# Attention on one core: weighted sums in six bursts a unit, by a written-out order, and one ring of seven PSUM banks

## The chip, the cores and the metric

The kernel runs on one core of one Trainium2 chip. The metric is the device time of an execution in microseconds (us). The engines are named as in the profile: PE (TensorE matmuls), PEld (TensorE weight loads), DVE (VectorE), ACT (ScalarE), POOL (GpSimd), SP (SyncE, which issues most DMAs).

## The reference

A parallel block over one sequence of 2048 rows of width 448: the input, plus multi-query attention (16 heads of width 28 that share one key and one value head), plus an MLP that normalises its input once more.

```python
S, D, H, Dh, F = 2048, 448, 16, 28, 1792
xn = layernorm(x)
q = (xn @ wq)  # 16 heads of 28
k, v = xn @ wk, xn @ wv  # one head each
p = softmax(q k^T * Dh ** -0.5)
A = (p v, heads side by side) @ wo
B = gelu(layernorm(xn) @ w1 + b1) @ w2 + b2
return x + A + B
```

## The kernel before, in words

The program has three stages. The first normalises the input and projects it to q, k and v. The second is the MLP, whose result, with the input and the second bias added, goes to a DRAM buffer `ad` (line 604). The third, attention, is the one that the change rewrites, and it lasts from about 352 us to the end.

**Units.** Attention is cut into 16 units. A unit is 512 query rows (a chunk `c`, four of them) and a group `g` of four heads. Of a unit there are 16 key tiles `kt` of 128 keys, and for each key tile four score products, one a head `j`: 64 a unit.

**Scores and exps.** `scores` (line 616) takes a PSUM bank, multiplies a key tile with one head's queries into it (line 618, one 128x512 matmul; the trace names the two kinds of bank `s` and `t`), and ScalarE writes the exponentials to an SBUF tile `p` (line 620). The queries carry an extra row that subtracts an estimate of the row maxima. Banks come from `score_bank` (line 613): by turns from `ring_a` (three banks, `s`) and from `ring_b` (three banks, `t`), so a score waits for the exp of the score six before it. The first eight scores (`EARLY`) run while the MLP's last matmuls run.

**Weighted sums.** `pv(u, kt)` (line 729) multiplies the four `p` tiles of a key tile with the values and a column of ones, each into its own 32 partitions of one bank `po` (line 733). The program has four such matmuls a key tile; the trace shows each of them twice, so that a burst of two key tiles stands there as x16. After 16 key tiles `po` holds the unit's unnormalised result and its denominators.

**Normalising.** `norm_jobs` (line 707) has three pieces. The first: DVE copies `po` to `oc` (line 710), and a DMA takes the denominators out of it (`rc`, line 712). The second: DVE saves them in `sums`, takes reciprocals (lines 714 and 715), and DMAs spread these through DRAM (`ld`, line 716) to all partitions (`tr`, four DMAs, line 719). The third: DVE multiplies (line 721) and rounds (`oth`, line 723), POOL makes the rest `otl` (line 724).

**Output projection.** `o_parts` (line 691) takes a unit's four row tiles in turn: three 128x448 matmuls into one bank (lines 696, 698, 700), then DVE adds the bank to a row tile that was loaded from `ad` (line 702). For the last head group the row tile goes out (line 704). The bank is the pool `mo`, which has one bank. It also serves `block_max` (line 537), which `find_max` runs once a unit for the next unit: a matmul (line 539), then on DVE a transpose, a maximum, a negation and a transpose back (lines 540 to 546), and a DMA of the row into the next unit's queries (line 547).

**The order.** Attention runs in steps of eight scores, eight steps a unit. At the end of each step stands a burst of two key tiles' weighted sums, those of the step before. Other jobs are put at a step and at a slot among its eight scores (`at`, line 768): the load of the next unit's queries at a unit's first step (`load_unit`, line 549: `qm` by four DMAs, then `xh` by four), the maxima at its fourth, and the matmuls of the output projection one at a time by the table `PARTS`, from the fifth step of the unit after on. All DMAs but two at the very end are issued by SP, in program order.

**The end.** `last_norm` (line 736) normalises the last unit without DMAs and adds its rows. `flag` checks that no denominator lies outside limits; if one does, a branch that is not taken here computes attention again.

PSUM has eight banks. In attention they are six for scores, one `mo`, one `po`. During the MLP they are three of `ring_a`, `mo`, and four that the MLP accumulates in.

Of the kernel before, what the change touches and what calls it, by code (L numbers as in the profile page):

```python
# [10 lines left out]
F32 = mybir.dt.float32  # L11
F32R = mybir.dt.float32r
I32 = mybir.dt.int32
# [3 lines left out]
PSUM = bass.MemoryType.PSUM  # L17

P = 128
S, D, H, DH, F = 2048, 448, 16, 28, 1792  # L20
NT = S // P
CT = 4
NCH = NT // CT
CW = CT * P
# [7 lines left out]
HD = D // 2  # L32
WEIGHTS = 28
EARLY = 8
PARTS = 2, 1, 2, 1, 2, 2, 2
LIMITS = 0.25, 2.0 ** 40


# [1 line left out]
def block_kernel(ctx, tc, x, wq, wk, wv, wo, w1, b1, w2, b2, out):  # L40
# [4 lines left out]
    def f(t):  # L45
        return t.bitcast(F32)

    keep = ctx.enter_context(tc.tile_pool(name="keep", bufs=1))
    mo = ctx.enter_context(tc.tile_pool(name="mo", bufs=1, space=PSUM))
    dram = ctx.enter_context(tc.tile_pool(name="dram", bufs=1, space=bass.MemoryType.DRAM))  # L50
    xt_p = ctx.enter_context(tc.tile_pool(name="xt", bufs=len(KEPT)))
    xl_p = ctx.enter_context(tc.tile_pool(name="xl", bufs=len(KEPT)))
# [56 lines left out]

    def mtile(shape):  # L110
        return mp.tile(shape, F32, name="m")

    def bank(shape):
        return mo.tile(shape, F32, name="mo")

    def rawtile(shape):
        return tmp.tile(shape, F32, name="raw", bufs=2)
# [116 lines left out]
    def second_of_first():  # L234
        ts = slice(0, CT)
        r = rstd(lnrq[:, 1:2, ts], lnp[:, ts, 1], CT, (True,))
        next(r)
        yield
        next(r)
        shift(True, ts)  # L240
        yield
# [199 lines left out]
    g = stats(1)  # L441
# [16 lines left out]
    g = second_of_first()  # L458
# [13 lines left out]
    for c in range(NCH):  # L472
        if c + 1 < NCH:
            center, turn = norm_parts(c + 1, False, bank=lambda shape: (qbank, mtile)[next(turns) % 2](shape))
        for i in range(4):
# [16 lines left out]
            if (c, i) == (NCH - 1, 3):  # L492
                _, end = evac()
# [6 lines left out]
            if i in ((1, 3), (1, 2), (1, 3), (0, 2))[c]:  # L500
                n = 2 * c + (i - 1 if c == 1 else i // 2 if c == 3 else i // 3)
# [12 lines left out]
    units = [(c, g) for c in range(NCH) for g in range(NG)]  # L514
    NU = len(units)
# [18 lines left out]
    def blocks(t):  # L534
        return t.rearrange("p (a b) -> p a b", b=32)

    def block_max(keys, dst):
        pm = bank([P, CW])
        pe.matmul(pm, keys, qm, start=True, stop=True)  # L539
        dve.transpose(tm, pm)  # L540
        dve.tensor_reduce(dst, blocks(tm), axis=AX.X, op=ALU.max)
# [7 lines left out]
    def load_unit(u):  # L549
        qss[u] = qst[u % 2]  # L550
        load_strips(u)
        load_q(u, qss[u])

    def find_max(u):
        mr = keep.tile([P, CW // 32], F32, name="mr", bufs=2)
        block_max(kd, mr)
        shift_rows(u, mr)

    ring_a = ctx.enter_context(tc.tile_pool(name="ra", bufs=3, space=PSUM))

    def spare():
        return ring_a.tile([P, CW], F32, name="s")
# [46 lines left out]
    turn_s = itertools.count()  # L609
    ring_b, ps = [], {}  # L610
    todo = [(u, kt, j) for u in range(NU) for kt in range(NT) for j in range(4)]

    def score_bank():
        return ring_b[0].tile([P, CW], F32, name="t") if ring_b and next(turn_s) % 2 else spare()

    def scores(u, kt, j):
        s = score_bank()
        pe.matmul(s, ks[:, kt * P:(kt + 1) * P], qss[u][:, j, :], start=True, stop=True)  # L618
        p = early.pop(0) if early else att.tile([P, CW], F32, name="p", bufs=WEIGHTS)
        act.activation(p, s, AF.Exp, scale=SCALE)  # L620
        ps[u, kt, j] = p
# [3 lines left out]
    for c in range(len(KEPT), NCH):  # L625
        g = norm_gen(MLP_ORDER[c], lambda shape: ring_a.tile(shape, F32, name="s"))
        for i in range(2 * CT + 1):
            norms[NF * (c - 1) + 4 + i] = lambda g=g: next(g, None)
    for n in range(len(mslots) + 2):
        c, ft = mslots[n] if n < len(mslots) else (NCH, n - len(mslots))  # L630
# [24 lines left out]
        if n >= len(mslots):  # L655
            t = f(xl_p.tile([P, 4, CW], F32R, name="xl"))
# [33 lines left out]

    def o_parts(c, g):
        oth, otl = ots[c, g]
        for k in range(CT):
            po = bank([P, D])
            ts = slice(k * P, (k + 1) * P)
            pe.matmul(po, oth[:, ts], woh[:, g, :], start=True, stop=False)  # L696
            yield
            pe.matmul(po, oth[:, ts], wol[:, g, :], start=False, stop=False)  # L698
            yield
            pe.matmul(po, otl[:, ts], woh[:, g, :], start=False, stop=True)  # L700
            a = rows[c, k]
            dve.tensor_add(a, a, po)  # L702
            if g == NG - 1:
                nc.sync.dma_start(ov[:, CT * c + k, :], a)
            yield

    def norm_jobs(u, po):
        c, g = units[u]
        oc = att.tile([P, CW], F32, name="oc")
        dve.tensor_copy(oc, po)  # L710
        rc = att.tile([P, CW // 32], F32, name="rc")
        nc.sync.dma_start(rc, oc[0:P:32, :])
        yield
        dve.tensor_copy(sums[:, u, :], rc)
        dve.reciprocal(rc, rc)
        nc.sync.dma_start(ld.rearrange("h (i e) -> (h i) e", e=CW // 32), rc)
        tr = att.tile([P, CW], F32, name="tr")
        for h in range(4):
            nc.sync.dma_start(tr[32 * h:32 * h + 32, :], ld[h:h + 1, :].to_broadcast([32, CW]))
        yield  # L720
        dve.tensor_mul(oc, oc, tr)
        oth, otl = ots[c, g] = [att.tile([P, CW], F32R, name=n, bufs=3) for n in ("oth", "otl")]
        dve.tensor_copy(oth, oc)
        pool.tensor_sub(otl, oc, f(oth))  # L724
        yield

    pos = {}

    def pv(u, kt):
        if kt == 0:  # L730
            pos[u] = op.tile([P, CW], F32, name="po")
        for j in range(4):
            pe.matmul(pos[u][32 * j:32 * j + 32, :], vs[:, kt, :], ps[u, kt, j],  # L733
                      start=(kt == 0), stop=(kt == NT - 1))
# [28 lines left out]
                dve.tensor_add(a, a, outs[k][:, 0:D])  # L763
            (nc.scalar if k % 2 else nc.sync).dma_start(ov[:, CT * c + k, :], a)

    side = {}

    def at(step, job, slot=4):
        side.setdefault((min(step, PER * NU - 1), slot), []).append(job)

    PER = NT // 2
    for u in range(NU):
        c, g = units[u]
        if u + 1 < NU:
            at(PER * u, lambda u=u: load_unit(u + 1))
            at(PER * u + 3, lambda u=u: find_max(u + 1))
        if g == 0:
            at(PER * (u + 1), lambda c=c: load_rows_of(c))
    at(3, split_out)
    waiting = []  # L780

    def weighted():
        for u, kt in waiting:
            pv(u, kt)
        if not waiting or waiting[-1][1] < NT - 1 or u == NU - 1:
            return
        norm = norm_jobs(u, pos.pop(u))
        next(norm)
        for d in (1, 3):
            at(PER * (u + 1) + d, lambda: next(norm), 3)  # L790
        parts = []

        def part():
            if not parts:
                parts.append(o_parts(*units[u]))
            next(parts[0])

        for d, n in enumerate(PARTS if u < NU - 2 else (3, 3, 3, 3)):
            for slot in (1, 5, 7)[:n]:
                at(PER * (u + 1) + 4 + d, part, slot)  # L800

    bad = keep.tile([P, 2], F32, name="bad")
    worst = keep.tile([P, 2], F32, name="worst")
# [3 lines left out]
    def extremes(src, to):  # L807
        dve.tensor_reduce(to[:, 0:1], src, axis=AX.X, op=ALU.max)
        dve.tensor_reduce(to[:, 1:2], src, axis=AX.X, op=ALU.min)

    def flag(last):
        extremes(last.bitcast(I32), bad)
        dve.tensor_tensor(bad[:, 0:1], bad[:, 0:1], worst[:, 0:1], op=ALU.max)
        dve.tensor_tensor(bad[:, 1:2], bad[:, 1:2], worst[:, 1:2], op=ALU.min)
        dve.tensor_scalar(bad[:, 0:1], bad[:, 0:1], hi, 0.0, op0=ALU.is_gt, op1=ALU.add)
        dve.scalar_tensor_tensor(bad[:, 0:1], bad[:, 1:2], lo, bad[:, 0:1], op0=ALU.is_lt, op1=ALU.add)
        pf = bank([1, 1])
        pe.matmul(pf, bad[:, 0:1], one[:, 0:1], start=True, stop=True)
        return lambda: dve.tensor_copy(count, pf)

    done = EARLY
    for step in range(PER * NU):
        for i in range(8):
            if done:
                done -= 1
            else:
                scores(*todo.pop(0))
            for job in side.pop((step, i), []):
                job()
        weighted()  # L830
        waiting = [divmod(n, NT) for n in (2 * step, 2 * step + 1)]
    extremes(sums[:, 0:NU - 1, :].rearrange("p u e -> p (u e)").bitcast(I32), worst)
    weighted()
    last_norm(NU - 1, pos.pop(NU - 1), flag)

    outside = nc.values_load(count)
# [47 lines left out]
```

## Time and profile before

| | |
|---|---|
| three runs | 906.68, 907.39 and 907.75 us |
| median | 907.39 us |
| the profiled execution's own time | 906.84 us |
| its span, from first to last instruction | 905.0 us |
| TensorE clock that the throttle granted, mean | 0.996 of full speed |
| PE busy, share of the span | 98% |
| ACT busy | 75% (32.19 us of a steady unit's 33.97) |
| DVE, POOL busy | 32%, 17% |

The span is what the profile covers; the execution's own time is 1.8 us longer. Matmuls are pipelined, and their lengths overlap: what a matmul costs on PE is read from the distance of the starts. A row of the timeline names the engine, the line of the kernel, and output<-inputs. A weight load (PEld) has a row of its own beside the matmul that it serves; it stands with the same line.

### The profile page before, as it was taken

Reading aid. Unit: us, or ns where it says so; the run is one execution under the profiler, and the core shown is the slowest. Engines: PE = TensorE matmul, PEld = TensorE weight load, DVE = VectorE, ACT = ScalarE, POOL = GpSimd, SP = SyncE. Lnnn points to the kernel's source line nnn. Section 1 sums busy time; section 2 is a strip of 40 time slices with the busy share of each in tenths; the row PEclk is TensorE's granted clock in tenths of the full one; section 3 lists DMA queues with packets and bytes.
Section 4 is the critical chain, followed back from the end, with each engine's and each line's share of the span. In section 5 each row is a group of like instructions: output and inputs, shape, how many; then the busy total and the mean of one; then the engine's idle time right before and its main releaser. Section 6 shows DMA issues by size and latency. Waiting matters only on the chain.

```text
span 905.0 us, 13020 instructions
## 1 busy us (share of the span) xinstructions
PE 891.2 (98%) x4925; PEld 567.7 (63%) x4925; DVE 294.0 (32%) x554; ACT 676.5 (75%) x1285; POOL 156.1 (17%) x149
## 2 busy tenths in 40 slices
PE   9989999999999999999999999999999999999996
PEld 8867888888888887454554554554554554554552
DVE  7865454334344442222122122122122122122113
ACT  5764443333443337999999999999999999999993
POOL 6443243243235331000000000000000000000000
PEclk9999999999999999999999999999999999999998
DMA  9791112002002204312202222202221202222001
GB/s 279 219 282 51 42 62 82 1 1 81 21 21 57 66 12 114 106 24 54 52 24 54 86 72 54 52 24 54 89 68 54 53 24 54 81 76 54 1 13 43
DMA packets 42041, 60.03 MB, mean 66 GB/s; under 512 B 10794, under 2 KB 26744, under 8 KB 41976
## 3 DMA queue, kind: packets, MB, share of 16 engines
q1 hardware_dynamic: 40568, 58.60, 22.9%
q8 instruction: 40, 0.66, 0.3%
q10 hardware_dynamic: 1408, 0.57, 0.2%
q14 instruction: 25, 0.20, 0.1%
HBM read 43.16 MB, written 14.80 MB: 64 GB/s over the span
## 4 chain that ended last, share of the span: by engine, by line
PE 94%; DVE 2%; ACT 2%; issue 1%; DMA 0%; POOL 0%; ACTq 0%; DVEq 0%; POOLq 0%
PE po L733 26%; PE s L618 16%; PE m L598 14%; PE t L618 13%; PE s L180 11%; PE qp L180 3%; PE mo L696 1%; PE mo L698 1%; PE mo L700 1%; PE s L185 1%; PE s L183 1%; PE qp L304 1%; DVE hz L581 0%; PE mo L539 0%; DVE hx L583 0%
## 5 line engine op out<-in xcount | busy, mean ns | idle before, releaser
L620 ACT ACTIVATE p<-s 128x512 f32<-128x512 f32 x508 | 315.5, 621 | 26.7 <-PE s L618 22.4
L620 ACT ACTIVATE p<-t 128x512 f32<-128x512 f32 x508 | 319.5, 629 | 0.0
L733 PE MATMUL po<-p,vs 128*32 128x512 f32 x2032 | 244.1, 598 | 0.0
L618 PE MATMUL s<-xh,ks 128*128 128x512 f32 x516 | 216.6, 420 | 0.0
L618 PE MATMUL t<-xh,ks 128*128 128x512 f32 x508 | 200.4, 395 | 0.2 <-DVE a L603 0.2
L618 PEld LDWEIGHTS s<-xh,ks 128*128 128x128 f32 x516 | 97.0, 188 | 121.6 <-ACT p L620 105.6
L733 PEld LDWEIGHTS po<-p,vs 128*32 128x32 f32 x2032 | 53.1, 109 | 121.5 <-issue 116.1
L579 ACT ACTIVATE hx<-s,b1t 128x512 f32<-128x512 f32 x56 | 38.5, 688 | 113.8 <-PE s L185 104.2
L702 DVE TENSOR_TENSOR row<-row,mo 128x448 f32<-128x448 f32 x60 | 37.3, 621 | 235.7 <-PE mo L700 234.5
L587 POOL TENSOR_TENSOR hl<-hx,hh 128x512 fp32r<-128x512 f32 x56 | 77.5, 1384 | 183.2 <-DVE hh L586 174.2
L724 POOL TENSOR_TENSOR otl<-oc,oth 128x512 fp32r<-128x512 f32 x15 | 19.3, 1289 | 500.6 <-PE t L618 236.5
L618 PEld LDWEIGHTS t<-xh,ks 128*128 128x128 f32 x508 | 95.5, 188 | 14.0 <-ACT p L620 1.9
L598 PE MATMUL m<-w2l,hh 128*128 128x448 f32 x224 | 82.6, 369 | 0.9 <-DVE w2l L382 0.9
L598 PE MATMUL m<-w2h,hh 128*128 128x448 f32 x224 | 82.4, 368 | 0.5 <-DVE a L603 0.4
L598 PE MATMUL m<-w2h,hl 128*128 128x448 f32 x224 | 82.0, 366 | 0.7 <-POOL hl L587 0.7
L581 DVE SCALAR_TENSOR_TENSOR hz<-hz,hx 128x512 f32<-128x512 f32 x56 | 45.4, 811 | 104.6 <-ACT hz L580 104.4
L582 ACT ACTIVATE hz<-hz 128x512 f32<-128x512 f32 x56 | 35.4, 632 | 49.8 <-DVE hz L581 49.8
L180 PE MATMUL s<-xh,w1h 128*128 128x512 f32 x168 | 65.7, 391 | 2.4 <-DVE qe L405 2.4
L180 PE MATMUL s<-xl,w1h 128*128 128x512 f32 x168 | 65.8, 392 | 0.0
L180 PE MATMUL s<-xh,w1l 128*128 128x512 f32 x168 | 65.8, 391 | 0.0
L583 DVE SCALAR_TENSOR_TENSOR hx<-hz,hx 128x512 f32<-128x512 f32 x56 | 39.1, 698 | 43.3 <-ACT hz L582 43.3
L710 DVE COPY oc<-po 128x512 f32<-128x512 f32 x15 | 10.4, 692 | 115.4 <-PE po L733 115.4
(162 smaller groups left out, 896.8 us busy)
## 6 DMA issues: line engine op xcount, KB each, us to landing
xh<-qd SPq DMA_DIRECT2D x64, 224.0 KB
qd<-qe SPq DMA_DIRECT2D x24, 256.0 KB
a<-in_A_x_dram SPq DMA_DIRECT2D x24, 224.0 KB
tr<-ld SPq DMA_DIRECT2D x60, 64.0 KB
ad<-a SPq DMA_DIRECT2D x16, 224.0 KB
qm<-qd SPq DMA_DIRECT2D x64, 56.0 KB
row<-ad SPq DMA_DIRECT2D x16, 224.0 KB
raw<-in_B_w_dram SPq DMA_DIRECT2D x7, 448.0 KB
```

The lines of the kernel that those rows point to most:

```text
L180: pe.matmul(ps, w, v, start=(n == 0), stop=False)
L579: act.activation(hx, ph, AF.Identity, bias=b1t[:, ft:ft + 1])
L581: dve.scalar_tensor_tensor(hz, hz, 1.0, hx, op0=ALU.add, op1=ALU.mult)
L582: act.activation(hz, hz, AF.Tanh, scale=GELU[1])
L583: dve.scalar_tensor_tensor(hx, hz, 1.0, hx, op0=ALU.add, op1=ALU.mult)
L587: pool.tensor_sub(hl, hx, f(hh))
L598: pe.matmul(m2[k], h[:, k * P:(k + 1) * P], w[:, ft, :], start=(ft == 0 and i == 0), stop=(ft == NF - 1 and i == 2))
L618: pe.matmul(s, ks[:, kt * P:(kt + 1) * P], qss[u][:, j, :], start=True, stop=True)
L620: act.activation(p, s, AF.Exp, scale=SCALE)
L702: dve.tensor_add(a, a, po)
L724: pool.tensor_sub(otl, oc, f(oth))
L733: pe.matmul(pos[u][32 * j:32 * j + 32, :], vs[:, kt, :], ps[u, kt, j], start=(kt == 0), stop=(kt == NT - 1))
```

## The change

The table `PARTS` and the steps go. The order of a unit is written out in `ORDER`, a string of tokens: `s7` is seven scores, `P2` is the weighted sums of two key tiles, `o` is a whole row tile of the output projection (all three matmuls and the add), `m` is the maxima of the next unit. A unit has 64 scores, 16 key tiles, 4 row tiles and one `m` as before, and its weighted sums come as P2, P3, P2, P3, P3, P3. Scores run eight ahead, as before.

The pieces of `norm_jobs` are placed by key tiles now: the first behind a unit's 16th, the second two key tiles later, the third six later, and the row tiles join the queue of `o` tokens eight later. So a unit's row tiles are spread over the next two units: two on the last two `o` of the next one, two on the first two `o` of the one after. Unit 0 has none, unit 1 only the last two. In the last unit an `o` takes up to four row tiles.

The pool `mo` goes. `ring_a` has four banks instead of three, and scores, maxima, row tiles and the final check all take banks from one ring of seven (four `s`, then three `t`), so each waits for the user of the bank seven before it. In the MLP stage `ring_a` alone is there, with four banks.

`load_unit` and `load_rows_of` stand ahead of a unit's order. `split_out`, two DVE operations that split the projection's weights, moves in unit 0 from behind the first maxima to behind the token `s9`, ahead of them.

```diff
-PARTS = 2, 1, 2, 1, 2, 2, 2
+ORDER = "s7 P2 s9 P3 s4 o s o s9 P2 m s9 P3 s9 P3 s3 o s9 P3 s4 o"
...
-    mo = ctx.enter_context(tc.tile_pool(name="mo", bufs=1, space=PSUM))
...
     def block_max(keys, dst):
-        pm = bank([P, CW])
+        pm = score_bank()
...
-    ring_a = ctx.enter_context(tc.tile_pool(name="ra", bufs=3, space=PSUM))
+    ring_a = ctx.enter_context(tc.tile_pool(name="ra", bufs=4, space=PSUM))
...
     def score_bank():
-        return ring_b[0].tile([P, CW], F32, name="t") if ring_b and next(turn_s) % 2 else spare()
+        return ring_b[0].tile([P, CW], F32, name="t") if ring_b and next(turn_s) % 7 > 3 else spare()
...
-            po = bank([P, D])
+            po = score_bank()[:, 0:D]
             ts = slice(k * P, (k + 1) * P)
             pe.matmul(po, oth[:, ts], woh[:, g, :], start=True, stop=False)
-            yield
             pe.matmul(po, oth[:, ts], wol[:, g, :], start=False, stop=False)
-            yield
             pe.matmul(po, otl[:, ts], woh[:, g, :], start=False, stop=True)
...
     def weighted():
-        for u, kt in waiting:
-            pv(u, kt)
...
+        n = next(place)
+        u, kt = divmod(n, NT)
+        pv(u, kt)
+        if kt == NT - 1 and u < NU - 1:
+            norm = norm_jobs(u, pos.pop(u))
+            next(norm)
+            soon(n + 2, lambda: next(norm))
+            soon(n + 6, lambda: next(norm))
+            soon(n + 8, lambda: parts.append(o_parts(*units[u])))
+        for job in at.pop(n, ()):
+            job()
...
+    def soon(n, job):
+        at.setdefault(n, []).append(job)
...
+    def part():
+        if parts and next(parts[0], True):
+            parts.pop(0)
+            part()
...
+    def token(kind, u):
+        if kind == "s" and todo:
+            scores(*todo.pop(0))
+        elif kind == "P":
+            weighted()
+        elif kind == "m" and u + 1 < NU:
+            find_max(u + 1)
+        elif kind == "m":
+            extremes(sums[:, 0:u, :].rearrange("p u e -> p (u e)").bitcast(I32), worst)
+        elif kind == "o":
+            for _ in range(CT if u == NU - 1 else 1):
+                part()
...
-        pf = bank([1, 1])
+        pf = score_bank()[0:1, 0:1]
...
+    for u in range(NU):
+        if u + 1 < NU:
+            load_unit(u + 1)
+        if units[u][1] == 0:
+            load_rows_of(units[u][0])
+        for n, word in enumerate(ORDER.split()):
+            for _ in range(int(word[1:] or 1)):
+                token(word[0], u)
+            if (u, n) == (0, 2):
+                split_out()
```

First place, PE in a steady unit. Before, a step of eight scores with two single projection matmuls, from one burst to the next:

```order
L733 MATMUL po<-p,vs 32x512 x8
L618 MATMUL s<-xh,ks 128x512
L618 MATMUL t<-xh,ks 128x512
L696 MATMUL mo<-xl,oth 128x448
L618 MATMUL s<-xh,ks 128x512
...
L698 MATMUL mo<-xl,oth 128x448
...
L733 MATMUL po<-p,vs 32x512 x8
```

Now, in the same engine's list, the stretch `P3 s4 o s o s9 P2 m` of a steady unit:

```order
L727 MATMUL po<-p,vs 32x512 x12
L614 MATMUL s<-xh,ks 128x512 x4
L692 MATMUL t<-xl,oth 128x448
L693 MATMUL t<-xl,oth 128x448
L694 MATMUL t<-xl,otl 128x448
L614 MATMUL t<-xh,ks 128x512
...
L614 MATMUL s<-xh,ks 128x512 x4
L614 MATMUL t<-xh,ks 128x512 x3
L614 MATMUL s<-xh,ks 128x512 x2
L727 MATMUL po<-p,vs 32x512 x8
L535 MATMUL s<-qm,kd 128x512
```

Bursts of 8 matmuls behind every eighth score became bursts of 8 or 12 with 9, 11 or 14 scores between them; the three matmuls of a row tile stand together, in a bank of the scores' ring, and so does the matmul of the maxima (L535).

Second place, DVE in a steady unit. Before, between the copy of `po` and the maxima (`oc`, `sums`, `rc` and `oth` belong to the normalising, `row` to the adds of the projection, `tm` and `mr` to the maxima):

```order
L710 COPY oc<-po 128x512
L702 TENSOR_TENSOR row<-row,mo 128x448
L714 COPY sums<-rc 128x16
L715 RECIPROCAL rc<-rc 128x16
L702 TENSOR_TENSOR row<-row,mo 128x448
L721 TENSOR_TENSOR oc<-oc,tr 128x512
L723 CAST oth<-oc 128x512
L540 STREAM_TRANSPOSE tm<-mo 128x512
```

Now:

```order
L704 COPY oc<-po 128x512
L696 TENSOR_TENSOR row<-row,t 128x448
L708 COPY sums<-rc 128x16
L709 RECIPROCAL rc<-rc 128x16
L696 TENSOR_TENSOR row<-row,t 128x448 x2
L715 TENSOR_TENSOR oc<-oc,tr 128x512
L717 CAST oth<-oc 128x512
L536 STREAM_TRANSPOSE tm<-s 128x512
```

One more add stands ahead of the multiplication that waits for `tr`, and the transpose behind it reads a bank of the ring instead of `mo`.

Third place, SP's queue of DMAs over a steady unit. Before:

```order
L547 DMA xh<-tm 1x4x512
L532 DMA qm<-qd_73 28x512 x4
L526 DMA xh<-qd_73 28x4x512 x2
L526 DMA xh<-qd_74 28x4x512 x2
L712 DMA rc<-oc 128x1x16
L716 DMA ld<-rc 128x16
L719 DMA tr<-ld 32x512 x4
```

Now:

```order
L543 DMA xh<-tm 1x4x512
L706 DMA rc<-oc 128x1x16
L528 DMA qm<-qd_70 28x512 x4
L522 DMA xh<-qd_70 28x4x512 x2
L522 DMA xh<-qd_71 28x4x512 x2
L710 DMA ld<-rc 128x16
L713 DMA tr<-ld 32x512 x4
```

The eight loads of the next unit's queries moved from ahead of `rc` to between `rc` and `ld`.

More of the change, by code (lines that the diff above doesn't have):

```diff
@@ L111, in mtile @@
         return mp.tile(shape, F32, name="m")
-    def bank(shape):
-        return mo.tile(shape, F32, name="mo")
     def rawtile(shape):
@@ L764, in last_norm @@
             (nc.scalar if k % 2 else nc.sync).dma_start(ov[:, CT * c + k, :], a)
[L766 to L780, printed above, removed]
-    def weighted():
-        for u, kt in waiting:
-            pv(u, kt)
[L785 to L800, printed above, removed]
+    at, parts, place = {}, [], itertools.count()
+    def soon(n, job):
+        at.setdefault(n, []).append(job)
+    def weighted():
+        n = next(place)
[25 more added lines that the diff above has]
+                part()
     bad = keep.tile([P, 2], F32, name="bad")
@@ L816, in flag @@
         dve.scalar_tensor_tensor(bad[:, 0:1], bad[:, 1:2], lo, bad[:, 0:1], op0=ALU.is_lt, op1=ALU.add)
-        pf = bank([1, 1])
+        pf = score_bank()[0:1, 0:1]
         pe.matmul(pf, bad[:, 0:1], one[:, 0:1], start=True, stop=True)
         return lambda: dve.tensor_copy(count, pf)
[L821 to L833, printed above, removed]
+    for u in range(NU):
[8 more added lines that the diff above has]
+                split_out()
     last_norm(NU - 1, pos.pop(NU - 1), flag)
```

## The prediction

> **What bounds the kernel now.** I read the chain of work that ended last on the page first, then a table by stretches, then the timeline of the attention stage.
>
> ```profile
> PE 94%; DVE 2%; ACT 2%; issue 1%; DMA 0%; POOL 0%; ACTq 0%; DVEq 0%; POOLq 0%
> ```
>
> The chain is TensorE nearly throughout, so what shortens its queue shortens the run, unless a wait takes its place. The stretches below (us, then busy us and count for PE, PEld, DVE, ACT, POOL, then clock and DMA) are unit 0, whose weighted sums run beside no output projection, and a steady unit.
>
> ```profile
> 354.24:386.08 31.84, 31.84 (x194) 14.92 (x193) 5.98 (x7) 31.56 (x65) 0.00 (x0) 1.00 0.50 126
> 419.73:453.70 33.97, 33.97 (x206) 17.10 (x205) 7.02 (x13) 32.19 (x66) 1.29 (x1) 1.00 0.17 43
> ```
>
> ScalarE is a close second: busy 32.19 of 33.97 us in a steady unit, 31.56 of 31.84 in unit 0. Next, one step of a steady unit in the timeline (start, length, engine, line, output<-input): 8 scores, 2 single matmuls of the output projection (mo), 1 burst of weighted sums (po), and the exps on ACT.
>
> ```profile
> 504.57 1.92 PE L733 MATMUL po<-p,vs 128*32 128x512 f32 x16
> ...
> 506.43 0.50 PE L618 MATMUL s<-xh,ks 128*128 128x512 f32 x1
> 506.76 0.40 PE L618 MATMUL t<-xh,ks 128*128 128x512 f32 x1
> 506.96 0.60 ACT L620 ACTIVATE p<-s 128x512 f32<-128x512 f32 x1
> 506.99 0.37 PE L696 MATMUL mo<-xl,oth 128*128 128x448 f32 x1
> 507.20 0.39 PE L618 MATMUL s<-xh,ks 128*128 128x512 f32 x1
> 507.20 0.19 PEld L618 LDWEIGHTS t<-xh,ks 128*128 128x128 f32 x1
> 507.43 0.39 PE L618 MATMUL t<-xh,ks 128*128 128x512 f32 x1
> 507.45 0.59 ACT L620 ACTIVATE p<-t 128x512 f32<-128x512 f32 x1
> ...
> 508.56 0.39 PE L618 MATMUL t<-xh,ks 128*128 128x512 f32 x1
> 508.88 1.92 PE L733 MATMUL po<-p,vs 128*32 128x512 f32 x16
> 510.32 0.67 ACT L620 ACTIVATE p<-t 128x512 f32<-128x512 f32 x1
> 511.27 0.60 ACT L620 ACTIVATE p<-s 128x512 f32<-128x512 f32 x1 [0.29 <-PE s L618]
> ```
>
> Starts count here, since lengths overlap. Scores start 0.23 apart (507.20, 507.43), a projection matmul takes 0.21 (506.99 to 507.20), exps start 0.48 apart (507.45 to 510.32 is six steps). The last burst of all has four key tiles instead of two:
>
> ```profile
> 887.90 3.64 PE L733 MATMUL po<-p,vs 128*32 128x512 f32 x32
> ```
>
> 3.64 less 1.92, by two, is 0.86 us a key tile, and it shows that a longer burst keeps that pace.
>
> **Part 1, fewer bursts.** The step from 504.57 to 508.88 lasts 4.31. Less 8 x 0.23, 2 x 0.21 and 2 x 0.86 leaves 0.33, which belongs to the burst itself: 0.09 ahead of it (508.56 to 508.88 is 0.32, not 0.23), 0.14 inside (504.57 to 506.43 is 1.86, not 1.72), 0.10 behind its first score (506.43 to 506.76 is 0.33, not 0.23). Before, 128 steps give 127 bursts (the first step has none). The changed order has 6 a unit, 96 in all. 31 x 0.33 = 10.2 us less; the counts of scores, key tiles, projection matmuls and maxima stay.
>
> **Part 2, waits for banks that go.** With the one mo bank, a row tile's first matmul waits for the add that empties it, once a unit, where DVE copies po first:
>
> ```profile
> 520.14 0.62 DVE L702 TENSOR_TENSOR row<-row,mo 128x448 f32<-128x448 f32 x1
> 520.86 0.42 PE L696 MATMUL mo<-xl,oth 128*128 128x448 f32 x1
> 521.12 0.39 PE L618 MATMUL s<-xh,ks 128*128 128x512 f32 x1
> ```
>
> The mo matmul holds PE 0.26, not 0.21: 0.05 x 14 units = 0.7 less. Steps without projection also wait, for one of six score banks:
>
> ```profile
> 369.19 0.59 ACT L620 ACTIVATE p<-t 128x512 f32<-128x512 f32 x1
> ...
> 369.83 0.19 PEld L618 LDWEIGHTS t<-xh,ks 128*128 128x128 f32 x1 [0.22 <-ACT p L620]
> 369.88 0.44 PE L618 MATMUL t<-xh,ks 128*128 128x512 f32 x1
> 370.25 1.07 PE L733 MATMUL po<-p,vs 128*32 128x512 f32 x8
> ```
>
> 369.88 to 370.25 is 0.37, not 0.32: 0.05 x some 9 steps = 0.5 less. The row also prices such a wait: the weight load starts 0.05 after the exp's end (369.78), and a load with nothing ahead costs 0.10 (as behind a burst), so a score runs 0.15 after its bank's exp has ended. At the stage's start the second score waits for MLP banks:
>
> ```profile
> 351.52 0.63 PE L618 MATMUL s<-xh,ks 128*128 128x512 f32 x2
> 352.40 0.50 PE L618 MATMUL t<-xh,ks 128*128 128x512 f32 x1 [0.25 <-DVE a L603]
> ```
>
> Now four s banks come first. The 0.42 lost there (0.65 since the score at 351.75) goes, and about 0.2 comes back as a wait for the last early exp: 0.2 less.
>
> **Part 3, waits that come: the ring of seven.** From these rows, in a run behind a burst, with ScalarE caught up, score k starts at 0.33 + 0.23 (k-2). The first exp starts 0.53 in (506.43 to 506.96), lasts 0.60, and the next follow 0.48 apart. Score k needs the bank of score k-7, free at 0.53 + 0.60 + 0.15 + 0.48 (k-8). For the 9th that is 1.76 against 1.94: no wait. For the 10th it is 2.24 against 2.17, and each later one adds 0.25. Row tiles of 0.62 stretch a run: in `s4 o s o s9` the last score is due at 0.33 + 12 x 0.23 + 1.24 = 4.33, and its bank, that of the 7th score, is free at 4.16. So a steady unit has no wait, with 0.17 to spare. But unit 0 has no row tiles and unit 1 not its first two: runs of 14, 12 and 11 in unit 0 cost 1.07 + 0.57 + 0.32, the run behind the short burst that follows 0.2, unit 1's run of 14 another 1.07. The last unit, where four row tiles stand together and no maxima part a burst from a run, I put at 0.3. Sum 3.5 more. The last burst needs exps of the last scores: 0.1 more.
>
> Here a rule speaks against the change. The rows have exps 0.48 us apart. The Trainium skill's page "ScalarE: Activation LUTs" (What ACT_TABLE_LOAD costs) gives an ACTIVATE with immediate scale and bias 186 ns plus 0.833 ns an element, neighbours overlapping by about 93 ns; that makes an estimate of 0.52 us here, 33.3 us a unit, and by it the ring would bind everywhere and the sum would be about 911. The trace does not agree: seven starts in a row at 0.48.
>
> **Part 4, DVE and its queue.** A row tile's bank and the maxima's are now ring banks, held until DVE has read them. An add ends some 1.4 us after its row tile begins (two matmuls of 0.21, the third's 0.37, the add's 0.62); the bank's next turn comes after 0.62 + 6 x 0.23 = 2.0 or later: hidden. The maxima stand behind `oc*tr` on DVE, and that waits for a chain of DMAs:
>
> ```profile
> 519.37 0.69 DVE L710 COPY oc<-po 128x512 f32<-128x512 f32 x1 [7.04 <-PE po L733]
> 524.64 0.17 DVE L714 COPY sums<-rc 128x16 f32<-128x16 f32 x1 [3.88 <-DMA rc<-oc]
> 530.28 0.69 DVE L721 TENSOR_TENSOR oc<-oc,tr 128x512 f32<-128x512 f32 x1 [4.03 <-DMA tr<-ld]
> 531.35 0.71 DVE L540 STREAM_TRANSPOSE tm<-mo 128x512 f32<-128x512 f32 x1
> ...
> 517.20 2.94 SPq L526 DMA_DIRECT2D xh<-qd  x4
> 520.23 0.57 SPq L712 DMA_DIRECT2D rc<-oc  x1
> 525.13 0.34 SPq L716 DMA_DIRECT2D ld<-rc  x1
> 526.56 1.98 SPq L719 DMA_DIRECT2D tr<-ld  x4
> 534.39 1.68 SPq L532 DMA_DIRECT2D qm<-qd  x4
> ```
>
> SP's queue now has the next unit's qm and xh between rc and ld. From the end of a unit's last burst: copy done 0.9, rc issued 1.6, qm and xh 6.3, ld lands at 7.8 (525.13 to 526.56 is 1.4), tr issued 9.8, landed 11.5 (530.28 less 528.54 is 1.7). The maxima's matmul comes at 16.7 (two runs of 11 and 9, bursts of 2 and 3, the run of 14, a burst of 2, by the prices above), its bank is needed again 1.7 later, at 18.4, and DVE needs 1.07 + 0.71 + 0.15 behind tr: spare until tr lands at 16.4. In the three units that load rows too, four more issues of xh's size take some 2.9: 14.4, still hidden; I put it at nothing, with 3 us for these units in the range. Before, the same waits stood ahead of the maxima, but held only mo. `split_out` goes ahead of the first maxima on DVE, where that engine was idle 9 us:
>
> ```profile
> 361.74 0.72 DVE L540 STREAM_TRANSPOSE tm<-mo 128x512 f32<-128x512 f32 x1 [9.40 <-PE mo L539]
> ```
>
> The MLP stage gains a fourth bank; no row there waits for one, so nothing. The tail behind the last burst keeps its operations.
>
> **Sum.** -10.2 - 0.7 - 0.5 - 0.2 + 3.5 + 0.1 = -8.0. The span of 905.0 becomes 897.0, the profiled execution's own 906.84 becomes 898.8. That execution lies 0.55 below the median of the three runs, 907.39; by the median it is 899.4, which I forecast.
>
> **The rivals.**
> - No ring waits (banks come free sooner, or ScalarE hurries): 3.6 less, 895.8. For it: the ring arithmetic rests on 0.15 for waking, from one row. Against: unit 0's ScalarE is already busy 31.56 of 31.84.
> - The ring binds in steady units too. Margins are 0.17, and lengths of exps climb from 0.59 to 0.67 within a step, so their ends are 0.49 apart. With 0.07 to 0.1 lacking in three or four of six runs, 0.2 to 0.4 a unit, 2.8 to 5.6 more: 902 to 905.
> - DVE holds the maxima's bank because tr lands 5 us later than laid out; at 0.5 a unit the gain is gone: 907. The longest rc wait, 3.88, speaks for late landings, but qm and xh are issued while it lasts.
> - The other side, ScalarE becomes the bound: if in long runs exps start 0.52 apart, 64 take 33.3, and six restarts with 0.1 to 0.2 idle (0.29 at 511.27) make 34.1 a unit against the 33.3 (33.97 less 0.66 and 0.05) that PE then needs: 0.8 x 14 = 11.2 more, 910.6, slower. It decides from about 0.515 on. Against it, the 0.48. It is what the Trainium skill's figure in Part 3 would make.
> - The 0.33 belongs to weight loads and not to bursts, so nothing is saved in Part 1: 909.6, slower. The Trainium skill's page "TensorE: Matmul & The Clock Gate" (Part 3, The mechanism) says that a weight load overlaps running matmuls only where the row group differs. The trace does not agree: at 507.20 a score's load of all rows starts with the score ahead of it and 0.23 before its own matmul.
>
> That the order isn't six bursts is no rival: the program's rows show them.
>
> **How the numbers follow.** Forecast 0.65 (897.5 to 901.5 by itself), no ring waits 0.13, ring binds 0.12, DVE 0.04, ScalarE 0.04, weight loads 0.02. The range from 895.8 to 903.5 leaves out the last three and half of the ring's. Within 0.2% (1.8 us, about what a measurement of this kernel can tell) lies only the DVE case: 0.04; slower 0.06; faster 0.90.
>
> **What would show it.** Right: 96 bursts, 0.33 apart from 0.23 behind each, steady units of 33.3 us, runs of 14 in units 0 and 1 whose last scores start 0.48 apart, waits on ScalarE there alone. Wrong: scores waiting in each unit on exps or on the maxima's transpose, a unit of 33.9 or more, or exps over 0.5 apart.

## The result, and the profile after

| | before | after |
|---|---|---|
| median | 907.03 us (906.51 to 907.75, 4 runs) | 946.03 us (945.20 to 946.93, 4 runs) |
| profiled execution: span | 905.0 us | 945.0 us |
| TensorE clock, mean | 0.996 | 0.994 |
| PE busy | 98% | 95% |
| first burst to last burst | 354.24 to 887.90, 533.66 us | 355.23 to 930.51, 575.28 us |

The ratio is 1.043 (95% interval 1.0411 to 1.0448): 39 us slower, where 8 us faster was forecast. The page of after, its head, its chain and the costliest groups on ACT (count, then busy us, mean ns of one, then idle time before them):

```profile
span 945.0 us, 13292 instructions
...
PE 80%; ACT 15%; DVE 2%; issue 2%; DMA 0%; POOL 0%; ACTq 0%; DVEq 0%; POOLq 0%
...
L616 ACT ACTIVATE p<-s 128x512 f32<-128x512 f32 x582 | 315.9, 676 | 41.5 <-PE s L614 41.4
L616 ACT ACTIVATE p<-t 128x512 f32<-128x512 f32 x434 | 245.4, 677 | 30.6 <-PE t L614 29.5
```

ACT has 15% of the chain instead of 2%, yet it idles 71 us waiting for scores (41.4 and 29.5). So PE waits for ACT and ACT for PE, in turn: no engine is the bound, their coupling is. PE's waits in the attention stage (us in total, times, longest):

```profile
PE t L614 <- ACT p L616: 18.6, 12, 2.0
PE s L614 <- ACT p L616: 15.2, 14, 1.5
```

Only 26 waits, of up to 2.0 us, about two a unit. The stretches of a steady unit, each from a burst's start to the next one's, tell where (columns as in the prediction). Their words are `s9 P3`, `s4 o s o s9 P2`, `m s9 P3`, `s9 P3`, `s3 o s9 P3` and `s4 o s7 P2`, each counted from the burst ahead:

```profile
571.49:575.67 4.18, 4.18 (x26) 2.03 (x25) 0.00 (x0) 4.18 (x10) 0.00 (x0) 1.00 0.58 163
575.67:583.07 7.40, 7.40 (x45) 4.36 (x44) 1.85 (x3) 7.03 (x16) 0.00 (x0) 1.00 0.38 88
583.07:589.35 6.28, 4.65 (x28) 2.14 (x27) 2.80 (x6) 6.18 (x13) 1.28 (x1) 1.00 0.00 1
589.35:595.65 6.30, 5.28 (x34) 2.22 (x34) 0.00 (x0) 4.11 (x9) 0.00 (x0) 1.00 0.01 3
595.65:602.00 6.35, 6.35 (x41) 3.42 (x41) 0.62 (x1) 4.76 (x11) 0.00 (x0) 1.00 0.00 0
602.00:608.08 6.08, 6.08 (x39) 3.15 (x39) 1.74 (x4) 5.72 (x13) 0.00 (x0) 1.00 0.07 17
```

Four of the six are full. The two behind the maxima `m`, the third and the fourth, leave PE idle 1.63 and 1.02 us. The timeline in the third:

```profile
583.07 1.92 PE L727 MATMUL po<-p,vs 128*32 128x512 f32 x16
584.93 0.50 PE L535 MATMUL t<-qm,kd 128*128 128x512 f32 x1
585.27 1.08 PE L614 MATMUL s<-xh,ks 128*128 128x512 f32 x4
585.47 0.72 DVE L536 STREAM_TRANSPOSE tm<-t 128x512 f32<-128x512 f32 x1 [1.85 <-PE t L535]
585.70 2.21 ACT L616 ACTIVATE p<-s 128x512 f32<-128x512 f32 x4
586.19 0.64 PE L614 MATMUL t<-xh,ks 128*128 128x512 f32 x2
587.62 0.77 ACT L616 ACTIVATE p<-t 128x512 f32<-128x512 f32 x1
588.45 0.50 PE L614 MATMUL t<-xh,ks 128*128 128x512 f32 x1 [1.63 <-ACT p L616]
```

The maxima take a `t` bank at 584.93; four `s` scores follow, then two `t` scores, and a third `t` score waits until 588.45. It starts 0.06 behind the end of the exp that began at 587.62 (0.77 long, so 588.39). ACT goes in order: four `s` exps, then the `t` exps, so that exp is of the score at 586.19, **two turns earlier**. By "the user of the bank seven before it" the third `t` score's bank is that of the maxima, and DVE had read it by 586.19 (585.47 + 0.72). A free bank lay unused, and the score waited for one just filled. So the sentence of the change that each waits for the user of the bank seven before it does not hold of the built program.

The built program says the same for the whole stage. How many takes later a bank of the ring is taken again (without the takes behind the last burst):

```text
after            2 turns x12   3 x17   6 x109   7 x909   8 x22   9 x1   21 to 25 x14
third piece later (below)              6 x20    7 x1044  8 x20
banks by name (below)                           7 x1084
```

Fourteen times a bank stays out for three rounds (21 to 25 takes); it is the maxima's, in every unit but the first. The others of its kind come round after two or three turns instead. In the kernel before, where in attention these pools serve the scores alone, they do hand out in turn (a bank is taken again after six takes, 1014 times of 1017). Here they don't. That a new tile gets the bank that the pool counts as free first when the program is built is my reading of why; it is inferred.

### The profile page after: what moved, and what is told of

It reads as the page before. It is cut to its first block, busy times and chain, and to the rows that moved or that the text cites. A ratio compares the mean times of both kernels' runs of the same rounds, so it can differ in the third digit from the quotient of the medians.

```text
span 945.0 us, 13292 instructions
## 1 busy us (share of the span) xinstructions
PE 895.7 (95%) x4925; PEld 572.1 (61%) x4925; DVE 293.9 (31%) x554; ACT 672.0 (71%) x1285; POOL 156.2 (17%) x149
## 4 chain that ended last, share of the span: by engine, by line
PE 80%; ACT 15%; DVE 2%; issue 2%; DMA 0%; POOL 0%; ACTq 0%; DVEq 0%; POOLq 0%
PE po L727 23%; PE m L594 14%; ACT p L616 13%; PE s L614 13%; PE s L176 11%; PE t L614 9%; PE qp L176 3%; PE s L181 1%; PE s L179 1%; PE qp L300 1%; DVE hz L577 0%; PE s L692 0%; PE s L693 0%; PE s L694 0%; PE t L692 0%
## 5 line engine op out<-in xcount | busy, mean ns | idle before, releaser
L616 ACT ACTIVATE p<-s 128x512 f32<-128x512 f32 x582 | 315.9, 676 | 41.5 <-PE s L614 41.4
L616 ACT ACTIVATE p<-t 128x512 f32<-128x512 f32 x434 | 245.4, 677 | 30.6 <-PE t L614 29.5
L727 PE MATMUL po<-p,vs 128*32 128x512 f32 x2032 | 240.6, 603 | 0.0
L614 PE MATMUL s<-xh,ks 128*128 128x512 f32 x590 | 186.0, 411 | 15.2 <-ACT p L616 15.2
L614 PEld LDWEIGHTS s<-xh,ks 128*128 128x128 f32 x590 | 108.0, 188 | 86.9 <-ACT p L616 41.2
L614 PE MATMUL t<-xh,ks 128*128 128x512 f32 x434 | 140.7, 410 | 18.6 <-ACT p L616 18.6
L727 PEld LDWEIGHTS po<-p,vs 128*32 128x32 f32 x2032 | 56.8, 110 | 126.6 <-issue 121.0
L614 PEld LDWEIGHTS t<-xh,ks 128*128 128x128 f32 x434 | 79.7, 188 | 71.5 <-ACT p L616 36.7
L696 DVE TENSOR_TENSOR row<-row,s 128x448 f32<-128x448 f32 x33 | 20.5, 621 | 167.2 <-PE s L694 167.2
L696 DVE TENSOR_TENSOR row<-row,t 128x448 f32<-128x448 f32 x27 | 16.8, 621 | 149.0 <-PE t L694 149.0
```

## The experiments

Ratios stand against runs of the kernel before on the same chip: its median was 906.79 us beside the first four, 907.57 beside the next four, 907.98 beside the last.

**Banks by name, a strict ring.** The two pools keep their banks, but each bank has a name of its own and they are taken in turn.

```diff
-    ring_a = ctx.enter_context(tc.tile_pool(name="ra", bufs=4, space=PSUM))
+    ring_a = ctx.enter_context(tc.tile_pool(name="ra", bufs=1, space=PSUM))
...
-        return ring_a.tile([P, CW], F32, name="s")
+        return ring_a.tile([P, CW], F32, name=f"s{next(turn_a) % 4}")
...
-        return ring_b[0].tile([P, CW], F32, name="t") if ring_b and next(turn_s) % 7 > 3 else spare()
+        return ring_b[0].tile([P, CW], F32, name=f"t{next(turn_b) % 3}") if ring_b and next(turn_s) % 7 > 3 else spare()
```

> The changed kernel with one edit: each of the seven banks is a pool entry of its own and they are taken strictly in turn, so each score, maxima and row tile waits for the user seven before it. In the changed kernel the pools hand a new tile the bank that they count as free first, and behind each unit's maxima that was a bank used two or three turns before. Theory A (the banks are handed out in a bad order): the two stretches behind the maxima fall from some 6.3 and 6.3 us to 4.4 and 5.0, units from 36.4 to 33.3 or 33.4, the time from 946 to 899 (897 to 902). Theory B (the maxima's bank really comes back late, since DVE stands behind the DMA of tr): the wait stays, now on DVE instead of ScalarE, 930 to 946. Theory C (runs of 9 with bursts of three make ScalarE too slow, its exps grew from 0.625 to 0.676 us): no change, 940 to 946.

908.53 us (906.12 to 909.97), ratio 1.0015 (1.0002 to 1.0027), span 906.0. Steady units last 33.42 and have no wait, so 37.5 us of the loss go with the hand-out of banks. But the three units that load rows last 34.98, 34.32 and 37.73: 6.8 more together. DVE, SP and PE in the third of them:

```profile
756.12 0.55 SPq L707 DMA_DIRECT2D rc<-oc  x1
...
760.28 2.37 SPq L686 DMA_DIRECT2D row<-ad  x4
762.75 0.73 SPq L711 DMA_DIRECT2D ld<-rc  x1
771.16 1.72 SPq L714 DMA_DIRECT2D tr<-ld  x4
774.46 0.69 DVE L716 TENSOR_TENSOR oc<-oc,tr 128x512 f32<-128x512 f32 x1 [5.75 <-DMA tr<-ld]
775.53 0.71 DVE L536 STREAM_TRANSPOSE tm<-s 128x512 f32<-128x512 f32 x1
776.30 1.57 PE L615 MATMUL s<-xh,ks 128*128 128x512 f32 x3 [2.45 <-DVE tm L536]
```

`ld` moves 8 KB, but behind the loads of queries and rows it lands 8.4 us after its issue (762.75 to 771.16). So `tr` lands 18.3 us after `rc`'s issue, DVE reaches the transpose late, and the score that needs the maxima's bank waits 2.45. In a strict ring that wait is real; in after it can't arise where the pools leave that bank out, and no wait of PE there is put down to DVE's transpose.

**The third piece of the normalising two key tiles later.** The pools stay as the change has them.

```diff
-            soon(n + 6, lambda: next(norm))
+            soon(n + 8, lambda: next(norm))
```

> The changed kernel with one edit: the third piece of the normalising (the multiplication that waits for tr, and oth) comes eight key tiles behind the unit's end instead of six, so it stands behind the maxima on DVE. Pools as in the changed kernel. Theory A, with the reason that the pools count the maxima's bank as late because DVE's work for it stands behind a wait for a DMA in the order made when the program is built: banks come back in turn, time 899 to 902. Theory B: the maxima's bank comes back early, also 899 to 902. Theory C: no change, 940 to 946. If A holds but the order of hand-outs has another reason: 940 to 946.

899.87 us (898.95 to 900.80), ratio 0.9923 (0.9906 to 0.9939), span 897.1. The two stretches behind the maxima, `m s9 P3` and `s9 P3`:

```profile
565.40:569.78 4.38, 4.38 (x27) 2.21 (x26) 1.88 (x4) 4.38 (x10) 0.00 (x0) 1.00 0.00 0
569.78:574.80 5.02, 5.02 (x34) 2.29 (x33) 1.41 (x3) 4.67 (x10) 1.29 (x1) 1.00 0.02 5
```

4.38 and 5.02 instead of 6.28 and 6.30; the unit is 33.42 instead of 36.59, and the banks' turns are seven, give or take one. With DVE's multiplication moved behind the maxima, nothing that waits for `tr` stands ahead of the transpose, and the pools hand out the maxima's bank again in time.

**Eight bursts on the strict ring**, with `m` behind the third burst.

```diff
-ORDER = "s7 P2 s9 P3 s4 o s o s9 P2 m s9 P3 s9 P3 s3 o s9 P3 s4 o"
+ORDER = "s8 P2 s8 P2 s4 o s2 o s2 P2 m s8 P2 s8 P2 s8 P2 s4 o s4 P2 s4 o s4 P2"
```

> The strict ring of the first of these kernels, with an order of eight bursts of two key tiles a unit and runs of eight scores, row tiles whole: s8 P2 s8 P2 s4 o s2 o s2 P2 m s8 P2 s8 P2 s8 P2 s4 o s4 P2 s4 o s4 P2. It prices a burst: 32 bursts more than with six. By 0.33 us a burst 10.2 more than the strict ring with six, less some 3.5 for the waits in units 0 and 1 that runs of eight don't have: 906 (904 to 908) if the strict ring gives 899. If the 0.33 belonged to weight loads and not to bursts: 896, faster than six bursts.

957.80 us (955.60 to 962.42), ratio 1.0575 (1.0545 to 1.0605). It was meant to price a burst and prices the other wait: here the maxima come earlier in a unit, while `tr` lands as late as ever, so DVE stands waiting ahead of the transpose in all 14 units behind the first, and `m s8 P2` lasts 5.1 to 11.6 us instead of the 4.15 of unit 0. DVE's and PE's waits:

```profile
DVE oc L716 <- DMA tr<-ld: 65.1, 14, 11.7
```

```profile
PE s L615 <- DVE tm L536: 20.8, 8, 6.7
PE t L615 <- DVE tm L536: 14.1, 6, 4.8
```

**Six bursts with the banks of before**: three `s` and three `t` in turn, `mo` for maxima and row tiles.

```diff
+    mo = ctx.enter_context(tc.tile_pool(name="mo", bufs=1, space=PSUM))
...
-        pm = score_bank()
+        pm = mo.tile([P, CW], F32, name="mo")
...
-    ring_a = ctx.enter_context(tc.tile_pool(name="ra", bufs=4, space=PSUM))
+    ring_a = ctx.enter_context(tc.tile_pool(name="ra", bufs=3, space=PSUM))
...
-        return ring_b[0].tile([P, CW], F32, name="t") if ring_b and next(turn_s) % 7 > 3 else spare()
+        return ring_b[0].tile([P, CW], F32, name="t") if ring_b and next(turn_s) % 2 else spare()
...
-            po = score_bank()[:, 0:D]
+            po = mo.tile([P, D], F32, name="mo")
...
```

> The order of the changed kernel with the banks of the kernel before: three and three for scores by turns, and one bank mo for the maxima and the row tiles. It takes the ring out of the change. Worked out from the exps' spacing of 0.48, a wake of 0.15 and the banks that this program has: runs of nine wait for a sixth bank, row tiles wait for mo's add, units of 35.9, time 943 (938 to 948). If six banks were enough and the ring alone is what lost the time: 899 to 905.

944.23 us (943.57 to 945.77), ratio 1.0409 (1.0390 to 1.0428); a steady unit 36.03. The end of a run of nine:

```profile
563.22 0.41 PE L615 MATMUL t<-xh,ks 128*128 128x512 f32 x1
563.62 0.49 PE L615 MATMUL s<-xh,ks 128*128 128x512 f32 x1
564.11 0.51 PE L615 MATMUL t<-xh,ks 128*128 128x512 f32 x1
564.54 1.92 PE L728 MATMUL po<-p,vs 128*32 128x512 f32 x16
```

From 563.22 on starts are 0.40, 0.49 and 0.43 apart (without a wait 0.23, and 0.32 ahead of a burst): six banks are too few for nine scores in a row. Row tiles wait for `mo` besides:

```profile
PE mo L693 <- DVE row L697: 9.2, 17, 0.7
```

Both were expected, and this run doesn't separate them. Each of the six stretches is longer than with seven banks in turn, by 0.25 to 1.0 us; that the time comes near the changed kernel's 946 is chance. The order needs the seventh bank, and needs it in turn.

**Strict ring and the piece later**, the two edits together.

> Strict ring of seven and the third piece of the normalising behind the maxima, both at once. The strict ring alone still waited for the maxima's bank in the three units that load rows (1.6, 0.9 and 4.3 us), the third piece alone came out at 899.9. If what is left of the loss is DVE behind the DMA of tr, both together give what the third piece alone gave, 899 to 900; if the strict ring costs something by itself, 903 to 908.

900.38 us (899.65 to 901.05), ratio 0.9922 (0.9909 to 0.9936); units of 33.39 to 33.42, the row-loading ones too, and no wait of PE from 360 to 880. So with both edits both waits are gone: the one that the hand-out made in after, and the one for `tr` that the strict ring had left.

**The same with eight bursts** (this and the order of the third experiment), now with nothing in DVE's way.

> As the one before it in this list, with eight bursts of two key tiles and runs of eight scores. The strict ring with eight bursts came out at 957.8, by DVE's waits for tr; with the third piece behind the maxima these should be gone in all units. Then only the price of a burst is left: 31 bursts more by 0.33 to 0.35 are 10.2 to 10.9, less some 3.5 to 4 of waits of long runs in units 0 and 1 and at the end: 6 to 7 above six bursts, 906 (904 to 908). If a burst has no price of its own: 896.

906.02 us (904.62 to 907.18), ratio 0.9985 (0.9976 to 0.9993), 5.6 above the last. Bursts of plain steps `s8 P2`:

```profile
551.09 1.92 PE L728 MATMUL po<-p,vs 128*32 128x512 f32 x16
555.01 1.92 PE L728 MATMUL po<-p,vs 128*32 128x512 f32 x16
```

3.92 a step; less 8 x 0.2335 and 2 x 0.858 (the prediction's 0.23 and 0.86, taken finer from the distances of the starts) that leaves 0.34 a burst, where 0.33 was forecast. A steady unit lasts 33.99 against 33.40: 0.59 for two bursts, so a burst is worth 0.30 over a unit. That it has a price of its own is shown: without one, 896 was expected. Over the program the 31 bursts more cost 5.6 and not 31 x 0.33, since this order has no runs of 11 to 14, whose waits the prediction put at 3.5; 6 to 7 was expected. In the two profiles 1.6 of the difference lies behind the last burst, where the granted clock was 0.60 instead of 0.86.

**The loads behind `tr`.** After, with pools and third piece as they are; the loads of queries and rows moved behind the token `P2`, so that `ld` and `tr` go ahead of them on SP.

```diff
-        if u + 1 < NU:
-            load_unit(u + 1)
-        if units[u][1] == 0:
-            load_rows_of(units[u][0])
...
+            if n == 1 and u + 1 < NU:
+                load_unit(u + 1)
+            if n == 1 and units[u][1] == 0:
+                load_rows_of(units[u][0])
```

> The changed kernel, its pools and its third piece as they are, with one edit: a unit's loads of queries and rows stand behind its first burst of two key tiles instead of ahead of the unit, so behind ld and tr in SP's queue. If the eight or twelve loads between rc and ld are what makes tr late, both effects go, the bad hand-outs (the order made at the build counts the maxima's bank as late) and the real waits: 899 to 901. If the place on DVE alone decides, whatever the queue: 940 to 946. If the loads now come too late for the maxima: a wait at the maxima's matmul, some 2 us a unit, 925 to 935.

899.64 us (899.28 to 901.37), ratio 0.9921 (0.9902 to 0.9939). SP and DVE in a row-loading unit:

```profile
752.27 0.56 SPq L706 DMA_DIRECT2D rc<-oc  x1
754.63 0.35 SPq L710 DMA_DIRECT2D ld<-rc  x1
756.06 1.72 SPq L713 DMA_DIRECT2D tr<-ld  x4
757.88 1.63 SPq L528 DMA_DIRECT2D qm<-qd  x4
...
764.78 0.68 DVE L715 TENSOR_TENSOR oc<-oc,tr 128x512 f32<-128x512 f32 x1
...
768.63 0.72 DVE L536 STREAM_TRANSPOSE tm<-s 128x512 f32<-128x512 f32 x1 [2.71 <-PE s L535]
```

`ld` lands 1.4 us after its issue, the multiplication waits for nothing, and DVE idles ahead of the transpose. This edit touches neither DVE's order nor the pools, and the banks go in turn again (with the same counts of turns as with the third piece later). Two edits repair the hand-out that share only this: they take the wait for `tr` further out of the transpose's way. On the chip it was out of the way in the unit shown of after (the multiplication at 582.46, the maxima's matmul at 584.93). That the pools go by a reckoning made when the program is built, in which DVE reads the maxima late, fits all of it; it is inferred, since no run opens that reckoning.

**Short runs in units 0 and 1**, on the kernel with strict ring and later piece: an order `FIRST` of their own for units that have no or few row tiles, with seven bursts and no run above 11.

```diff
+FIRST = "s7 P2 s9 P3 s9 P2 s9 P2 m s9 P3 s9 P2 s3 o s5 P2 s4 o"
...
-        for n, word in enumerate(ORDER.split()):
+        for n, word in enumerate((FIRST if u < 2 else ORDER).split()):
```

> Strict ring, third piece behind the maxima, and in units 0 and 1, which have few row tiles or none, an order of seven bursts with runs of nine (s7 P2 s9 P3 s9 P2 s9 P2 m s9 P3 s9 P2 s3 o s5 P2 s4 o). It prices the waits of the long runs that no row tile parts: about 3 us of them go, two bursts more cost 0.7: 1.8 to 2.4 less than six bursts throughout, 897 to 898. If those waits were not what the recurrence says: the same as six bursts throughout, or 0.7 more.

898.60 us (897.96 to 899.16), ratio 0.9903 (0.9888 to 0.9918), the fastest of all. From first to last burst it takes 527.69 (355.19 to 882.87) against 529.05 (355.23 to 884.28): 1.4 less with two bursts more. The medians are 1.8 apart, at the lower edge of the 1.8 to 2.4 expected, and the time lies above the expected 897 to 898. Each of these five times lies below each of the six without the edit on the same chip, but the intervals of the two ratios overlap.

**The maxima's bank kept back by hand.** The kernel with strict ring and later piece, with nothing in DVE's way, but the maxima's bank stays out while eight `t` or eleven `s` are taken. In the built program it comes back 22 to 26 takes later (21 to 25 in after), and 37 takes have a turn of two or three (29 in after).

```diff
+    free = {"s": [0, 1, 2, 3], "t": [0, 1, 2]}
+    kept = []
...
+        at = free[kind].pop(0)
+        if keep:
+            kept.append([kind, 11 if kind == "s" else 8, at])
+        else:
+            free[kind].append(at)
```

> The kernel with the strict ring and the third piece behind the maxima (900.4), with one thing put back by hand: the maxima's bank is kept out of its kind's rotation for two rounds (8 turns of t, 11 of s), and the others of that kind go round meanwhile. No DMA wait stands ahead of the maxima on DVE here, so nothing but the choice of banks can cost. The built program reuses a bank after two or three turns 37 times, where the changed kernel does so 29 times. Theory A, worked out with the same recurrence (0.48 between exps, 0.15 to wake): 45 us more, 945 (935 to 955), with the waits on ScalarE in the two stretches behind the maxima. If the loss of the changed kernel was rather DVE's waits for tr, which the strict ring had hidden in part: 900 to 910.

948.60 us (946.96 to 949.21), ratio 1.0447 (1.0428 to 1.0466), with after's waits:

```profile
PE t L631 <- ACT p L633: 19.6, 14, 2.0
PE s L631 <- ACT p L633: 18.0, 17, 1.5
```

So leaving out that bank, alone, costs 48 us over the same kernel with its banks in turn. With 37 short turns for after's 29 it is a little harsher than after, and it is enough for the whole loss.

## Why the prediction was wrong

**The step that failed** is in Part 3: "Score k needs the bank of score k-7". I took the ring from the words of the change and read the program's rows only for the order of instructions, where a tile stands as `s` or `t` without the bank behind it. The built program could have told it before any run: it has 29 takes in which a bank comes back after two or three turns. The step that rested on it, "a steady unit has no wait, with 0.17 to spare", put at nothing what cost most. With such a turn the same arithmetic gives the loss. ACT has a score's exp ready 0.53 + 0.60 + 0.15 behind it at the best, and later where its queue is full: the score of 586.19 was released at 588.39, 2.2 later, where PE wanted its bank 0.46 later. The prices of the step were right, only the number of turns was not. Over 14 units, the two stretches behind the maxima hold 45.5 us more than their 4.38 and 5.02; after takes 46.1 more from first to last burst than the kernel with the later piece (575.28 against 529.15).

**None of the rivals was it.** "The ring binds in steady units too" has the right waiter and releaser, but as a lack of 0.07 to 0.1 in three or four runs, not of 1.9 and 1.3 in two. "DVE holds the maxima's bank" has the right place; its wait is not in after, since the bank was left out, but it came with the strict ring. ScalarE as the bound was not it: in the rows above four exps start within 1.92 (585.70 to 587.62), 0.48 apart, with PE waiting for them. "No ring waits" is answered by the run of 14 below, and that the 0.33 belonged to weight loads by the eight bursts, 5.6 us slower than six. The rival that I dismissed in one sentence, that the change doesn't do what it says, was the one: I asked it of the bursts and not of the banks.

**Part 4** put the landing of `tr` too early. From `rc`'s issue it reckoned 10.4 us in a steady unit and 13.3 in a row-loading one; after took 13.3 in the steady unit shown, and the strict ring 18.3 in its third row-loading unit. The term that failed is `ld`, put at the 1.4 of before, where the loads had been issued 5.0 us ahead of it (517.20 + 2.94 against 525.13). In after:

```profile
569.12 0.55 SPq L706 DMA_DIRECT2D rc<-oc  x1
569.76 1.72 SPq L528 DMA_DIRECT2D qm<-qd  x4
571.59 2.79 SPq L522 DMA_DIRECT2D xh<-qd  x4
574.48 0.34 SPq L710 DMA_DIRECT2D ld<-rc  x1
578.99 1.70 SPq L713 DMA_DIRECT2D tr<-ld  x4
...
582.46 0.69 DVE L715 TENSOR_TENSOR oc<-oc,tr 128x512 f32<-128x512 f32 x1 [0.77 <-DMA tr<-ld]
```

`ld` took 4.5 us (574.48 to 578.99) behind four loads of 56 KB and four of 224 KB, and 8.4 in the strict ring with four of 224 KB more. With the loads moved behind it, it took 1.4 again. I counted the loads' time on SP's queue (the issues) and not the time until they have moved. In a steady unit the spare of 4.9 us covers it; in the three row-loading units it doesn't, and with the banks in turn "still hidden" cost 6.8 there.

**What held, and what was luck.** With the banks in turn a steady unit lasts 33.40 to 33.42, forecast 33.3, and the span with the later piece is 897.1, forecast 897.0. That the spans agree is luck, by two misses that cancel. From the start of the first burst to the end of the last, the kernel before took 537.3 us (354.24 to 891.55) and the one with the later piece 532.0 (353.55 to 885.52): 5.3 less, and 6.0 with the 0.7 by which the first burst came earlier, where the terms of the sum make 8.0. Most of what is missing lies in the steady units: they gained 0.57 and not 0.71. Two bursts are worth 0.59 and not 0.66, and the 0.05 for `mo` doesn't show, since eight bursts without it last 33.99, as long as a unit of before. The other 1.9 us came from the tail behind the last burst, which the prediction put at nothing: 13.5 us before, 11.6 with the later piece. There the granted clock was 0.72 before (half speed from 894.0 on, for 6.8 us) and 0.90 with the later piece; why it differs no run shows.

The waits of the long runs held well. The run of 14 in unit 0 of after:

```profile
362.10 0.73 PE L614 MATMUL s<-xh,ks 128*128 128x512 f32 x2
362.67 0.86 PE L614 MATMUL t<-xh,ks 128*128 128x512 f32 x3
363.37 1.10 PE L614 MATMUL s<-xh,ks 128*128 128x512 f32 x4
364.31 1.43 PE L614 MATMUL t<-xh,ks 128*128 128x512 f32 x3
365.73 0.99 PE L614 MATMUL s<-xh,ks 128*128 128x512 f32 x2
366.66 1.92 PE L727 MATMUL po<-p,vs 128*32 128x512 f32 x16
```

At 0.33 and then 0.23 apart the burst behind the run would come at 365.6; it comes at 366.66, since from 364.31 on the starts are 0.47 apart (three in 1.42), ACT's pace. That is 1.1; 1.07 was forecast.

## What to carry to other kernels

A pool with several banks is a ring only if the kernel makes it one: give the banks names and take them in turn, or read in the built program how many turns later each comes back, above all behind a tile with another reader than its neighbours'. Whatever an in-order engine has standing behind a wait for a DMA holds the banks that it has yet to read, so put such a wait behind the work that frees a bank. And let a chain of small DMAs go ahead of big loads on its queue, since a small one behind them lands late: 4.5 to 8.4 us after its issue here, 1.4 ahead of them.

## What the runs showed of the hardware

The length of an exp in the trace is not its cost: lengths rise to 0.85 us in long runs of exps, and their mean is 676 to 680 ns, in after as in the fast kernel with the later piece, while their starts stay 0.477 to 0.478 apart. The Trainium skill's page "ScalarE: Activation LUTs" (What ACT_TABLE_LOAD costs) would give an estimate of 0.52 by its figures; the runs don't agree with it, and the measured distance decides.

The first burst came at 355.23 in after and at 353.55 with the later piece, although they do the same until then. The clock granted between 60 and 100 us was 0.96 in the one and 1.00 in the other; 4% of 40 us is 1.6, nearly all of it. The profile of the fastest kernel, too, had 0.96 there.

A wait of PE can cost more than its length, since behind two of after's waits the granted clock fell: behind those that ended at 406.45 (1.95 long) and 625.52 (1.88), the next bursts took 3.42 us instead of 1.92 and 3.95 instead of 2.78. The stretches that these bursts begin lasted 8.50 and 7.71 us, at a mean clock of 0.80 and 0.84; the `s9 P3` shown above lasted 6.30 at 1.00. The other waits had no such drop, and no run here shows what decides it.
